# A gap's last product with w_out and the next visit's first product with w_in change places

## The chip, the cores and the metric

The kernel runs on one core of one Trainium2 chip. The metric is the device time of one execution in microseconds. The time before is the median of three runs; the profile is of one execution more.

## The reference

What is computed is an attention with two kinds of masks, followed by two layers of the same form, all in float32. In short:

```python
scores = (q @ k^T) / sqrt(D), masked: 4 heads local (32 keys), 4 heads strided (every 32nd key)
x = softmax(scores) @ v            # 4 x 576 tokens x 512
h = x @ w_in;  x = max(h, 0)**2 @ w_out      # layer 1: 512 -> 2048 -> 512
h = x @ w_in2; x = max(h, 0)**2 @ w_out2     # layer 2, the same shape
```

There are 2304 tokens. The change touches the second layer alone.

## The kernel before

Each float32 operand of a product is split into a high part and a rest, and a product is made as three matmuls: high by high, high by rest, rest by high. The second layer is worked off in blocks of tokens: one of 256 tokens (the narrow block) and then four of 512 (the wide blocks). In the wide blocks a 2 x 2 block product is made with seven products in place of eight, for w_in and for w_out alike.

A wide block runs over eight pairs q of column tiles of w_in (with the rows of w_out that belong to them). `pairs7` (line 1239) lists the 32 pairs (k, q) of the four blocks. `seven` (line 1518) runs over 31 of them and calls `frame` (line 1318) for each: `frame` makes the products with w_in of the pair that comes next (`nxt`) in four *visits*, and between them, in four *gaps*, the products with w_out of the present pair. So TensorE alternates in an order that is written out by hand:

- visit 1: products "11" and "s2" (12 matmuls), then gap 0 (9 matmuls),
- visit 2: product "12" (6 matmuls), then gap 1 (9),
- visit 3: products "s1" and "s3" (12), then gap 2 (15),
- visit 4: products "s4" and "22" (12), then gap 3 (9).

That is 84 matmuls a pair, each 128x128 by 128x256. A visit (`visit`, line 1273; the matmul is line 1279) takes weights as the stationary operand and x (from `xall`) as the moving one, and writes the PSUM tile `ps_m`. There is one such tile for the four visits of a pair, in the pool `ps_h` with one buffer (the third and fourth visit of the first pair of all take another). Its first matmul starts a new sum. After visit 1 ScalarE copies the tile out (line 1359); after visits 2, 3 and 4 VectorE reads it (`add`, lines 1111 and 1112). A gap's product (`n_unit`, line 1290; the matmul is line 1306) takes g, the squared positive part, as stationary operand (`ah`, `al`, `bh`, `bl`) and a unit of w_out from a ring of eight buffers as the moving one, and adds to a PSUM bank `banks[name]`. After the sixth matmul of a unit `ring_load` (line 1250) has SyncE load the ring's buffer with a later unit (line 1253).

The seven units of a pair come in the order of `ORDER` (line 1235): 11, 12, a22t4, s2t2, s1t1, s3t3, s4b22, six matmuls each. `n_unit` returns two closures of three matmuls each, and `seven` cuts the fourteen into the four gaps:

```python
todo = [one for name in ORDER for one in n_unit(k, q, name)]
gaps = todo[:3], todo[3:6], todo[6:11], todo[11:]
```

In the profile `MATMUL` on PE and its `LDWEIGHTS` on PEld are one product; a wait of a product stands at its weight load.

Of the kernel before, what the change touches and what calls it, by code (L numbers as in the profile page):

```python
# [17 lines left out]
P = 128  # L18
# [57 lines left out]
HALF = DM // 2  # L76
# [93 lines left out]
def tile_attention_then_two_mlps(  # L170
# [9 lines left out]
    nc = tc.nc  # L180
# [258 lines left out]
    for i in range(0, half2, 2):  # L439
        n = i + 2 if i + 2 < half2 else None  # L440
# [660 lines left out]
    def high(hi, src):  # L1101
        nc.scalar.activation(out=hi, in_=src, func=AF.Copy)  # L1102
# [95 lines left out]
    def x_op(k, i):  # L1198
        at = (k - NB) % 2 * 10 + 2 * i if i < 5 else 10 + 2 * i
        return [  # L1200
            xall[:, 48 + (at + a) * TB:48 + (at + a + 1) * TB].rearrange("p (c n) -> p c n", c=2)
            for a in range(2)
        ]
# [35 lines left out]
    pairs7 = [(k, q) for k in range(NB + 1, 2 * NB) for q in range(NF // 2)]  # L1239
# [5 lines left out]
    n_use, banks, acc, of = [0], {}, {}, {}  # L1245

    def ring(u):
        return wt["in", 1, 2 * (u % (NF // 2)) + 1][:, 0]
# [18 lines left out]
    def m_weights(q, name):  # L1267
        if name[0] == "s":
            return [t[:, int(name[1]) - 1] for t in s_parts[NF + 2 * q]]
        w = wt["in", 1, 2 * q + int(name[0]) - 1]  # L1270
        return [w[:, int(name[1]) - 1, a] for a in range(2)]

    def visit(k, q, ps, *products):
        for half, (name, i) in enumerate(products):
            w_hi, w_lo = m_weights(q, name)
            x_hi, x_lo = x_op(k, i)
            for j in range(2):
                for m, (w, x) in enumerate(((w_hi, x_hi), (w_lo, x_hi), (w_hi, x_lo))):
                    nc.tensor.matmul(  # L1279
                        ps[:, half * HT:(half + 1) * HT],  # L1280
                        lhsT=w[:, j * P:(j + 1) * P],
                        rhs=x[:, j],
                        start=half == 0 and j == 0 and m == 0,
                        stop=half + 1 == len(products) and j == 1 and m == 2,
                    )
# [4 lines left out]
    def n_unit(k, q, name):  # L1290
        first, end = q == 0, q == NF // 2 - 1
        if k == last7:
            end = q == NF // 2 - 2 and name not in ("12", "s4b22")
        u = n_use[0]
        n_use[0] += 1
        w_hi, w_lo = (ring(u)[:, a] for a in range(2))

        def half(t):
            if first and t == 0:
                tag = BANK.get(name, "a")  # L1300
                pool = ps_a if tag == "a" else ps_y
                banks[name] = pool.tile([P, 512], F32, tag=tag, name="ps_y")
            h, lo = g_op(name)
            rows = slice(t * P, (t + 1) * P)
            for m, (g, w) in enumerate(((h, w_hi), (h, w_lo), (lo, w_hi))):
                nc.tensor.matmul(  # L1306
                    banks[name][:, t * HALF:(t + 1) * HALF],
                    lhsT=g[:, rows],
                    rhs=w,
                    start=first and t == 0 and m == 0,  # L1310
                    stop=end and t == 1 and m == 2,
                )
            if t:
                ring_load(u + NF // 2)

        return [lambda t=t: half(t) for t in range(2)]

    def frame(gaps, nxt, cur, copies=((), (), ()), end=False, x=((), (), ()), late=()):

        k, q = nxt  # L1320
        if not of:
            of["r"] = gpool.tile([P, TB], F32, tag="r", name="r", bufs=1)
            of["c"] = gpool.tile([P, TB], F32, tag="sq", name="c", bufs=1)
            shapes = {"bh": ("qk0", 4), "bl": ("qk1", 4), "ah": ("qk2", 3)}
            for t, (tag, n) in shapes.items():
                of[t] = fpool.tile([P, n * HALF], F32R, tag=tag, name=t, bufs=1).rearrange(
                    "p (i n) -> p i n", i=n)
            for t, n in (("al", 2), ("al2", 1)):
                of[t] = gpool.tile([P, 3 * HALF], F32R, tag="gl", name=t, bufs=2)[
                    :, 48:48 + n * HALF].rearrange("p (i n) -> p i n", i=n)  # L1330
        r, c = (of[t].rearrange("p (h n) -> p h n", h=2) for t in ("r", "c"))
        a11, a22, a21, a12 = r[:, 0], r[:, 1], c[:, 0], c[:, 1]
        ah, al, bh, bl = (of[t] for t in ("ah", "al", "bh", "bl"))
        sums_x, high_x, rest_x = x

        def positive(t, src):
            nc.scalar.activation(out=t, in_=src, func=AF.Relu)
            nc.scalar.activation(out=t, in_=t, func=AF.Square)

        if cur:  # L1340
            s13, s24 = (
                gpool.tile([P, TB + P], F32, tag="gh", name="s", bufs=2)[:, :TB].rearrange(
                    "p (i n) -> p i n", i=2)
                for _ in range(2)
            )
            high(ah[:, 2], a12)
            tt(s13[:, 0], a21, a22, ALU.add)
            tt(s13[:, 1], a11, a21, ALU.subtract)
            rest(ah[:, 2], of["al2"][:, 0], a12)
            tt(s24[:, 0], s13[:, 0], a11, ALU.subtract)  # L1350
            tt(s24[:, 1], a12, s24[:, 0], ALU.subtract)
        each(copies[0])
        ps = ps_h.tile([P, TB], F32, tag="h", name="ps_m")
        visit(k, q, ps, ("11", 0), ("s2", 1))
        m, u = (vpool.tile([P, 512], F32, tag="val", name="u") for _ in range(2))

        c11, u2 = m[:, :HT], m[:, HT:]
        u3 = u[:, HT:]
        nc.scalar.activation(out=m, in_=ps, func=AF.Copy, scale=W_BACK)
        tt(u2, c11, u2, ALU.add)  # L1360
        each(copies[1])
        if cur:
            high(ah[:, 0:2], s13)
            high(bh[:, 2:4], s24)
        each(copies[2])
        each(gaps[0])
        if end:
            first_sum()
            rest(ah[:, 0:2], al, s13)
        visit(k, q, ps, ("12", 2))  # L1370
        add(c11, ps[:, :HT], c11)
        if cur:
            rest(bh[:, 2:4], bl[:, 2:4], s24)
        if cur and not end:
            rest(ah[:, 0:2], al, s13)
        each(sums_x)
        if end:
            each(high_x)
            each(rest_x)
        positive(a11, c11)  # L1380
        high(bh[:, 0], a11)
        if not end:
            each(high_x)
        each(gaps[1])
        if nxt == pairs7[0]:
            ps = ps_a.tile([P, TB], F32, tag="a", name="ps_m")
        visit(k, q, ps, ("s1", 3), ("s3", 4))
        add(
            u.rearrange("p (h n) -> p h n", h=2),
            ps.rearrange("p (h n) -> p h n", h=2),  # L1390
            u2.unsqueeze(1).to_broadcast([P, 2, HT]),
        )
        add(a22, ps[:, :HT], u3)
        positive(a22, a22)
        high(bh[:, 1], a22)
        rest(bh[:, 0], bl[:, 0], a11)
        if not end:
            each(rest_x)
        each(gaps[2])
        each(late)  # L1400
        rest(bh[:, 1], bl[:, 1], a22)
        visit(k, q, ps, ("s4", 5), ("22", 6))
        add(of["c"], ps, u)
        squares(of["c"])
        each(gaps[3])
# [110 lines left out]
            nc.sync.dma_start(out=rows_out(1, 1)[:, a], in_=halves(o)[:, a])  # L1516

    def seven():
        copies, sums = None, []
        for n, (k, q) in enumerate(pairs7[:-1]):  # L1520
            todo = [one for name in ORDER for one in n_unit(k, q, name)]
            gaps = todo[:3], todo[3:6], todo[6:11], todo[11:]
            end = q == NF // 2 - 1 or n + 2 == len(pairs7)
            more = k < last7
            x = [[], [], []]
            if more and q == 0:
                x_work[k + 1] = x_works(k + 1)
            if more and q > 1:
                x = [list(part) for part in x_work[k + 1][q - 2]]
            late = [lambda: sums_late(not more)] if end else []  # L1530
            if sums:
                first, then = sums.pop(0)
                x[0] += first
                late += then
            frame(gaps, pairs7[n + 1], True, copies or ((), (), ()), end, x, late)
            copies = None
            if more and q in (1, 2):
                load_x(k + 1, q - 1)
            if end and more:
                copies, sums = sums_then(k)  # L1540
        finish()
# [8 lines left out]
    with tc.manual_schedule():  # L1550
# [3 lines left out]
        ps = ps_h.tile([P, TB], F32, tag="h", name="ps_w")[:, :P]  # L1554
# [19 lines left out]
        for s in range(len(steps)):  # L1574
            k, f = steps[s]
            layer, j = blocks[k]
# [81 lines left out]
```

## Time and profile before

| | |
|---|---|
| median of 3 runs | 860.36 us (860.15 to 861.51) |
| the profiled execution | 861.31 us, its span 859.5 us |
| PE busy | 847.9 us, 99% of the span |
| PEld busy | 770.0 us, 90% |
| VectorE (DVE) busy | 681.6 us, 79% |
| ScalarE (ACT) busy | 525.8 us, 61% |

The page of the profile has the busy time of each engine, the span in 40 slices with the clock granted to TensorE, and groups of instructions by line. Ends of matmuls are modelled, so a busy PE doesn't say how closely its matmuls follow one another; their starts do. The loop that the change touches runs from about 557 us to 850 us.

### The profile page before, as it was taken

Reading aid. Unit: us, or ns where it says so; the run is one execution under the profiler, and the core shown is the slowest. Engines: PE = TensorE matmul, PEld = TensorE weight load, DVE = VectorE, ACT = ScalarE, POOL = GpSimd, SP = SyncE. Lnnn points to the kernel's source line nnn. Section 1 sums busy time; section 2 is a strip of 40 time slices with the busy share of each in tenths; the row PEclk is TensorE's granted clock in tenths of the full one; section 3 lists DMA queues with packets and bytes.
Section 4 is the critical chain, followed back from the end, with each engine's and each line's share of the span. In section 5 each row is a group of like instructions: output and inputs, shape, how many; then the busy total and the mean of one; then the engine's idle time right before and its main releaser. Section 6 shows DMA issues by size and latency. Waiting matters only on the chain. (4 is left out here: it accounts for less than half of the span.)

```text
span 859.5 us, 16041 instructions
## 1 busy us (share of the span) xinstructions
PE 847.9 (99%) x5719; PEld 770.0 (90%) x5719; DVE 681.6 (79%) x1710; ACT 525.8 (61%) x1216; POOL 17.5 (2%) x15
## 2 busy tenths in 40 slices
PE   8899999999999999999999999999999999999998
PEld 8778888888788888899888899999999999999998
DVE  5899896489775777478889996678888888888877
ACT  6987775467675666376766774455555564556442
POOL 0710000000000000000000000000000000000000
PEclk9999999999999999999999999999999999999999
DMA  8965721222222222268996476476668667766764
GB/s 257 348 216 157 239 64 45 88 78 76 73 78 98 61 71 59 74 245 295 348 364 213 157 265 239 130 225 202 188 202 281 186 194 236 238 187 198 229 188 132
DMA packets 82399, 155.21 MB, mean 181 GB/s; under 512 B 7568, under 2 KB 36368, under 8 KB 80272
## 3 DMA queue, kind: packets, MB, share of 16 engines
q1 hardware_dynamic: 82320, 154.19, 55.1%
q8 instruction: 45, 0.74, 0.3%
q14 instruction: 34, 0.28, 0.1%
HBM read 127.95 MB, written 26.21 MB: 179 GB/s over the span
## 5 line engine op out<-in xcount | busy, mean ns | idle before, releaser
L975 PE MATMUL ps_h<-xall,w 128*128 128x512 f32 (+1 forms) x1153 | 247.3, 358 | 0.0
L975 PEld LDWEIGHTS ps_h<-xall,w 128*128 128x128 f32 x1153 | 185.1, 188 | 26.0
L975 PE MATMUL ps_y<-gh,w 128*128 128x512 f32 (+1 forms) x640 | 155.7, 374 | 0.7 <-ACT gh L1024 0.7
L975 PEld LDWEIGHTS ps_y<-gh,w 128*128 128x128 f32 x640 | 107.9, 188 | 17.6 <-ACT gh L1024 1.1
L1279 PE MATMUL ps_m<-xall,s 128*128 128x256 f32 x768 | 104.5, 279 | 0.3 <-DVE r L1112 0.3
L1018 ACT ACTIVATE r<-ps_h 128x512 f32<-128x512 f32 x80 | 47.7, 597 | 86.9 <-PE ps_h L975 78.1
L1279 PEld LDWEIGHTS ps_m<-xall,s 128*128 128x128 f32 x768 | 95.5, 188 | 0.9 <-DVE r L1112 0.8
L1306 PE MATMUL ps_y<-w,bh 128*128 128x256 f32 x496 | 91.8, 278 | 0.0
L1279 PE MATMUL ps_m<-xall,w 128*128 128x256 f32 x576 | 83.4, 281 | 0.4 <-DVE c L1112 0.4
L975 PE MATMUL ps_y<-gl,w 128*128 128x512 f32 (+1 forms) x324 | 83.8, 370 | 0.0
L1306 PEld LDWEIGHTS ps_y<-w,bh 128*128 128x128 f32 x496 | 75.3, 188 | 0.0
L1279 PEld LDWEIGHTS ps_m<-xall,w 128*128 128x128 f32 x576 | 74.2, 188 | 1.1 <-DVE c L1112 0.6
L1029 DVE TENSOR_TENSOR gl<-sq,gh 128x512 fp32r<-128x512 f32 x80 | 55.3, 691 | 22.2 <-ACT gh L1024 17.5
L1306 PE MATMUL ps_y<-w,ah 128*128 128x256 f32 x372 | 70.0, 278 | 0.0
L1306 PE MATMUL ps_y<-w,bl 128*128 128x256 f32 x248 | 68.8, 277 | 0.0
L1027 DVE TENSOR_TENSOR sq<-r 128x512 f32<-128x512 f32 x38 | 26.3, 692 | 50.6 <-ACT r L1018 50.6
L975 PEld LDWEIGHTS ps_y<-gl,w 128*128 128x128 f32 x324 | 55.7, 188 | 9.6 <-DVE gl L1029 0.4
L1306 PEld LDWEIGHTS ps_y<-w,ah 128*128 128x128 f32 x372 | 56.7, 189 | 0.0
L1112 DVE SCALAR_TENSOR_TENSOR u<-ps_m,u 128x256 f32<-128x256 f32 x64 | 35.7, 557 | 25.5 <-PE ps_m L1279 25.4
L680 ACT ACTIVATE s<-s,m 96x128 f32<-96x128 f32 (+2 forms) x88 | 34.3, 390 | 34.2 <-DVE m L564 33.5
L1102 ACT ACTIVATE ah<-c 128x256 fp32r<-128x256 f32 x33 | 13.7, 418 | 63.4 <-DVE c L1288 63.4
L1306 PE MATMUL ps_y<-w,al 128*128 128x256 f32 x186 | 51.7, 278 | 0.0
(121 smaller groups left out, 1500.8 us busy)
## 6 DMA issues: line engine op xcount, KB each, us to landing
w<-w_mem SPq DMA_DIRECT2D x221, 256.0 KB, 2.8
raw<-moe_w_in_d SPq DMA_DIRECT2D x32, 512.0 KB, 5.7
raw<-moe_w_out_d SPq DMA_DIRECT2D x24, 512.0 KB, 5.2
w_mem<-xall SPq DMA_DIRECT2D x16, 512.0 KB, 3.9
w_mem<-xall SPq DMA_DIRECT2D x8, 1024.0 KB, 5.1
xall<-w_mem SPq DMA_DIRECT2D x8, 1024.0 KB, 5.4
qk<-loc_qk_d SPq DMA_DIRECT2D x12, 416.0 KB, 3.2
out_d<-o SPq DMA_DIRECT2D x17, 256.0 KB, 2.6
```

Source lines behind the costliest of these rows:

```text
L680: nc.scalar.activation(out=blk, in_=blk, func=AF.Exp, scale=-1.0, bias=m[:nq, j:j + 1], accum_out=dens[i][:nq, j:j + 1],)
L975: nc.tensor.matmul(y[:, c:c + w], lhsT=lhsT, rhs=rhs[:, c:c + w], start=start and c == 0, stop=stop and c + w == n,)
L1018: nc.scalar.activation(out=r, in_=ps, func=AF.Relu, scale=W_BACK)
L1027: nc.vector.tensor_tensor(out=sq, in0=r, in1=r, op=ALU.mult)
L1029: nc.vector.tensor_tensor(out=lo, in0=sq, in1=r32(h), op=ALU.subtract)
L1102: nc.scalar.activation(out=hi, in_=src, func=AF.Copy)
L1112: nc.vector.scalar_tensor_tensor(out=dst, in0=src, scalar=sign * W_BACK, in1=to, op0=ALU.mult, op1=ALU.add)
L1279: nc.tensor.matmul(ps[:, half * HT:(half + 1) * HT], lhsT=w[:, j * P:(j + 1) * P], rhs=x[:, j], start=half == 0 and j == 0 and m == 0, sto ...
L1306: nc.tensor.matmul(banks[name][:, t * HALF:(t + 1) * HALF], lhsT=g[:, rows], rhs=w, start=first and t == 0 and m == 0, stop=end and t == 1 ...
```

## The change

`n_unit` returns six closures of one matmul each, in the same order, and `ring_load` stays with the sixth. `seven` cuts the 42 into the same four gaps (9, 9, 15, 9). The last matmul of each gap is taken out of its gap and handed to the next visit as `between`; `visit` issues it after its own first matmul. The last of gap 3 goes to the first visit of the next call. Left as they were: the first visit of the first call (nothing comes from a gap of this loop), the second visit of the first call (`n == 0`), and the last call's gap 3.

```diff
--- before.py
+++ after.py
@@ -1270,12 +1270,14 @@
         w = wt["in", 1, 2 * q + int(name[0]) - 1]
         return [w[:, int(name[1]) - 1, a] for a in range(2)]
 
-    def visit(k, q, ps, *products):
+    def visit(k, q, ps, *products, between=None):
         for half, (name, i) in enumerate(products):
             w_hi, w_lo = m_weights(q, name)
             x_hi, x_lo = x_op(k, i)
             for j in range(2):
                 for m, (w, x) in enumerate(((w_hi, x_hi), (w_lo, x_hi), (w_hi, x_lo))):
+                    if half == 0 and j == 0 and m == 1 and between is not None:
+                        between()
                     nc.tensor.matmul(
                         ps[:, half * HT:(half + 1) * HT],
                         lhsT=w[:, j * P:(j + 1) * P],
@@ -1295,27 +1297,27 @@
         n_use[0] += 1
         w_hi, w_lo = (ring(u)[:, a] for a in range(2))
 
-        def half(t):
-            if first and t == 0:
+        def one(t, m):
+            if first and t == 0 and m == 0:
                 tag = BANK.get(name, "a")
                 pool = ps_a if tag == "a" else ps_y
                 banks[name] = pool.tile([P, 512], F32, tag=tag, name="ps_y")
             h, lo = g_op(name)
-            rows = slice(t * P, (t + 1) * P)
-            for m, (g, w) in enumerate(((h, w_hi), (h, w_lo), (lo, w_hi))):
-                nc.tensor.matmul(
-                    banks[name][:, t * HALF:(t + 1) * HALF],
-                    lhsT=g[:, rows],
-                    rhs=w,
-                    start=first and t == 0 and m == 0,
-                    stop=end and t == 1 and m == 2,
-                )
-            if t:
+            g, w = ((h, w_hi), (h, w_lo), (lo, w_hi))[m]
+            nc.tensor.matmul(
+                banks[name][:, t * HALF:(t + 1) * HALF],
+                lhsT=g[:, t * P:(t + 1) * P],
+                rhs=w,
+                start=first and t == 0 and m == 0,
+                stop=end and t == 1 and m == 2,
+            )
+            if t and m == 2:
                 ring_load(u + NF // 2)
 
-        return [lambda t=t: half(t) for t in range(2)]
-
-    def frame(gaps, nxt, cur, copies=((), (), ()), end=False, x=((), (), ()), late=()):
+        return [lambda t=t, m=m: one(t, m) for t in range(2) for m in range(3)]
+
+    def frame(gaps, nxt, cur, copies=((), (), ()), end=False, x=((), (), ()), late=(),
+              between=(None,) * 4):
 
         k, q = nxt
         if not of:
@@ -1351,7 +1353,7 @@
             tt(s24[:, 1], a12, s24[:, 0], ALU.subtract)
         each(copies[0])
         ps = ps_h.tile([P, TB], F32, tag="h", name="ps_m")
-        visit(k, q, ps, ("11", 0), ("s2", 1))
+        visit(k, q, ps, ("11", 0), ("s2", 1), between=between[0])
         m, u = (vpool.tile([P, 512], F32, tag="val", name="u") for _ in range(2))
 
         c11, u2 = m[:, :HT], m[:, HT:]
@@ -1367,7 +1369,7 @@
         if end:
             first_sum()
             rest(ah[:, 0:2], al, s13)
-        visit(k, q, ps, ("12", 2))
+        visit(k, q, ps, ("12", 2), between=between[1])
         add(c11, ps[:, :HT], c11)
         if cur:
             rest(bh[:, 2:4], bl[:, 2:4], s24)
@@ -1384,7 +1386,7 @@
         each(gaps[1])
         if nxt == pairs7[0]:
             ps = ps_a.tile([P, TB], F32, tag="a", name="ps_m")
-        visit(k, q, ps, ("s1", 3), ("s3", 4))
+        visit(k, q, ps, ("s1", 3), ("s3", 4), between=between[2])
         add(
             u.rearrange("p (h n) -> p h n", h=2),
             ps.rearrange("p (h n) -> p h n", h=2),
@@ -1399,7 +1401,7 @@
         each(gaps[2])
         each(late)
         rest(bh[:, 1], bl[:, 1], a22)
-        visit(k, q, ps, ("s4", 5), ("22", 6))
+        visit(k, q, ps, ("s4", 5), ("22", 6), between=between[3])
         add(of["c"], ps, u)
         squares(of["c"])
         each(gaps[3])
@@ -1516,10 +1518,17 @@
             nc.sync.dma_start(out=rows_out(1, 1)[:, a], in_=halves(o)[:, a])
 
     def seven():
-        copies, sums = None, []
+        copies, sums, kept = None, [], None
         for n, (k, q) in enumerate(pairs7[:-1]):
             todo = [one for name in ORDER for one in n_unit(k, q, name)]
-            gaps = todo[:3], todo[3:6], todo[6:11], todo[11:]
+
+            cuts = 0, 9, 18, 33, 42
+            gaps = [todo[a:b] for a, b in zip(cuts, cuts[1:])]
+            between = [kept] + [gap.pop() for gap in gaps[:3]]
+            if n == 0:
+                gaps[0].append(between[1])
+                between[1] = None
+            kept = gaps[3].pop() if n + 2 < len(pairs7) else None
             end = q == NF // 2 - 1 or n + 2 == len(pairs7)
             more = k < last7
             x = [[], [], []]
@@ -1532,7 +1541,7 @@
                 first, then = sums.pop(0)
                 x[0] += first
                 late += then
-            frame(gaps, pairs7[n + 1], True, copies or ((), (), ()), end, x, late)
+            frame(gaps, pairs7[n + 1], True, copies or ((), (), ()), end, x, late, between)
             copies = None
             if more and q in (1, 2):
                 load_x(k + 1, q - 1)
```

## Rows read from the trace of the kernel before

**Rows 1.** the page: busy us, share and instructions; granted clock in 40 slices

```profile
PE 847.9 (99%) x5719; PEld 770.0 (90%) x5719; DVE 681.6 (79%) x1710; ACT 525.8 (61%) x1216; POOL 17.5 (2%) x15
...
PEclk9999999999999999999999999999999999999999
```

**Rows 2.** the list of waits, 557 to 850 us: who, us in total, times, longest

```profile
PEld ps_m L1279 <- DVE c L1112: 0.6, 1, 0.6
```

**Rows 3.** the timeline of PE, 596 to 606 us: start us, us, line, tiles, count

```profile
596.03 0.85 PE L1279 MATMUL ps_m<-xall,w 128*128 128x256 f32 x6
...
597.41 0.39 PE L1306 MATMUL ps_y<-w,bh 128*128 128x256 f32 x2
...
598.43 0.87 PE L1279 MATMUL ps_m<-xall,w 128*128 128x256 f32 x6
599.14 0.40 PE L1306 MATMUL ps_y<-w,ah 128*128 128x256 f32 x2
...
600.20 1.54 PE L1279 MATMUL ps_m<-xall,s 128*128 128x256 f32 x12
601.57 0.39 PE L1306 MATMUL ps_y<-w,bh 128*128 128x256 f32 x2
...
603.27 0.87 PE L1279 MATMUL ps_m<-xall,s 128*128 128x256 f32 x6
...
604.69 0.40 PE L1306 MATMUL ps_y<-w,ah 128*128 128x256 f32 x2
...
605.75 0.52 PE L1279 MATMUL ps_m<-xall,w 128*128 128x256 f32 x3
```

**Rows 4.** the timeline, two first visits whose weight load waited

```profile
634.10 0.69 DVE L1112 SCALAR_TENSOR_TENSOR c<-ps_m,u 128x512 f32<-128x512 f32 x1
...
634.84 0.77 PEld L1279 LDWEIGHTS ps_m<-xall,w 128*128 128x128 f32 x6
...
732.09 0.68 DVE L1112 SCALAR_TENSOR_TENSOR c<-ps_m,u 128x512 f32<-128x512 f32 x1
...
732.83 0.30 PEld L1279 LDWEIGHTS ps_m<-xall,w 128*128 128x128 f32 x2 [0.64 <-DVE c L1112]
```

**Rows 5.** the timeline, an ordinary first visit: reader of ps_m and weight load

```profile
604.89 0.69 DVE L1112 SCALAR_TENSOR_TENSOR c<-ps_m,u 128x512 f32<-128x512 f32 x1 [0.15 <-PE ps_m L1279]
...
605.64 0.66 PEld L1279 LDWEIGHTS ps_m<-xall,w 128*128 128x128 f32 x5
```

**Rows 6.** the timeline, an ordinary second visit

```profile
597.61 0.60 ACT L1359 ACTIVATE u<-ps_m 128x512 f32<-128x512 f32 x1 [0.57 <-PE ps_m L1279]
...
598.32 0.30 PEld L1279 LDWEIGHTS ps_m<-xall,w 128*128 128x128 f32 x2
```

**Rows 7.** the timeline, an ordinary third and fourth visit

```profile
599.34 0.42 DVE L1112 SCALAR_TENSOR_TENSOR u<-ps_m,u 128x256 f32<-128x256 f32 x1 [0.48 <-PE ps_m L1279]
...
600.09 0.19 PEld L1279 LDWEIGHTS ps_m<-xall,s 128*128 128x128 f32 x1
...
602.50 0.42 DVE L1112 SCALAR_TENSOR_TENSOR r<-ps_m,u 128x256 f32<-128x256 f32 x1
...
603.16 0.30 PEld L1279 LDWEIGHTS ps_m<-xall,s 128*128 128x128 f32 x2
```

**Rows 8.** the timeline, the fourth visit and its gap at a block's end

```profile
632.42 0.65 PEld L1279 LDWEIGHTS ps_m<-xall,s 128*128 128x128 f32 x5
...
633.89 0.39 PE L1306 MATMUL ps_y<-w,ah 128*128 128x256 f32 x2
...
634.92 0.54 PE L1279 MATMUL ps_m<-xall,w 128*128 128x256 f32 x3
```

**Rows 9.** the page's DMA issues: KB each, median us to landing

```profile
w<-w_mem SPq DMA_DIRECT2D x221, 256.0 KB, 2.8
```

**Rows 10.** the timeline of PE, the same gap at another block's end

```profile
711.73 0.40 PE L1306 MATMUL ps_y<-w,ah 128*128 128x256 f32 x2
...
712.79 0.63 PE L1279 MATMUL ps_m<-xall,w 128*128 128x256 f32 x4
```

## The prediction

> **What bounds the kernel now.** I read the busy shares first, then the idle time of the stretch that the change touches, then single starts in it. On the page TensorE (PE) is busy 99% of the span and the clock row shows the full 2.4 GHz level everywhere [rows 1]. So only PE's own spacing, or a hole in its stream, can move the time. The changed loop runs from 557 us to 850 us. There the list of waits has next to nothing for PE: one wait of 0.6 us of a weight load [rows 2]. Every other engine waits for PE, not PE for it.
>
> Single starts show two things that the shares hide. I use starts alone, since ends of matmuls are modelled. A pair of the loop (84 products) runs from the first product of a visit at 596.03 to the same product at 605.75, 9.72 us [rows 3]; this repeats within 0.01 us in most pairs.
>
> First, **PE has two paces.** Differences of starts over counts of products [rows 3]: first visit 1.38 us for 12, its gap 1.02 for 9, second visit 0.71 for 6, its gap 1.06 for 9, third visit 1.37 for 12, its gap 1.70 for 15, fourth visit 1.42 for 12, its gap 1.06 for 9. That is 113 ns a product in a fast stretch and 118 in a slow one, at one granted clock. The pace changes only where a gap ends and a visit begins, there at each of the four visits; from a visit into its gap it stays. So 36 products of 84 run slow (6 + 9 + 12 + 9). At 1.02/9 and 1.06/9 the difference is 4.4 ns, so slow stretches cost 36 x 4.4 = 0.16 us a pair. The rest, 9.72 - 84 x 0.1133 - 0.16 = 0.04 us, lies at the eight borders between visits and gaps, some 5 ns each.
>
> Second, **the first weight load of a visit is hardly early.** A visit's first product overwrites the PSUM tile of the visit before it, so its weight load waits until VectorE or ScalarE has read that tile. How long after the reader's end the load can start is seen where it had to wait: reader 634.10 + 0.69 = 634.79, load 634.84; and 732.09 + 0.68 = 732.77, load 732.83 [rows 4]. I take 0.05 us. In the ordinary pair, first visit: reader 604.89 + 0.69 = 605.58, load 605.64: 0.06 us, so no slack that I can read [rows 5]. Second visit: ScalarE 597.61 + 0.60 = 598.21, load 598.32: slack 0.11 - 0.05 = 0.06 [rows 6]. Third: 599.34 + 0.42 = 599.76, load 600.09: slack 0.28. Fourth: 602.50 + 0.42 = 602.92, load 603.16: slack 0.19 [rows 7].
>
> **The change part by part.** No product, load, DMA or byte is added or removed; the products of a gap are cut one by one instead of by threes, which changes no instruction. In a pair with all swaps the order at four places goes from "gap's last, visit's first, visit's second" to "visit's first, gap's last, visit's second". Swapped are the third and fourth visit of 31 pairs and the first and second of 30 (the first pair has no gap of the loop ahead of it and its second visit is left alone; the last pair's closing gap feeds no visit): 122 places.
>
> *What the swap does to the wait.* The last product of a visit keeps its place, so the tile's reader starts and ends as before. The load of the next visit's first product moves up by one product, and everything behind it on PE's queue (the gap's product and the visit's rest) stands behind its wait.
> - First visit: its load moves up by one slow product, 0.12 us, from 605.64 to 605.52 [rows 5]; it can go at 605.58 + 0.05 = 605.63. Wait 0.11 us x 30 = 3.3 us. In the blocks' first pairs a wait is there already (634.84 above); there the same 0.11 is added, so the count stands.
> - Second visit: it moves up by one fast product, 0.11, from 598.32 to 598.21, and can go at 598.21 + 0.05 = 598.26 [rows 6]: 0.05 us x 30 = 1.5 us. If its gap ran slow, the gap would be 0.04 longer, and 0.01 would be left.
> - Third and fourth: slack 0.28 and 0.19 against 0.11, so nothing [rows 7]. At the end of a block the fourth already waits: its twelve products take from about 632.43 (load 632.42) to 633.89, 1.46 us, some 0.1 more than the 1.37 of a fast twelve [rows 3, 8]. Three such places, 0.11 each: 0.3 us.
> Sum of waits: 5.1 us. What hides an earlier product elsewhere is only this slack; there is no other work for PE behind a waiting load.
>
> *What else moves.* The gap's product that is passed ends up to 0.11 us later, plus the wait. Two of the four (ahead of visits three and one) carry the issue of the weight ring's next DMA on SyncE; the ring holds eight units and a pair uses seven, so the unit loaded is used more than a pair later, over 9.7 us, and a load lands in 2.8 us [rows 9], so nothing waits. The passed product's g operand has 0.11 us more time. VectorE and ScalarE follow PE, and shift with it.
>
> *What it does to the paces.* No row of before shows a single visit product between two gap products, so I bound it. At best all products run at the fast pace: minus 0.16 us a pair and minus the slips at the changes. At worst all run slow: 48 x 4.4 ns = plus 0.21 us. In between lies "as many slow as now": 0. What rows say of the middle: a fourth visit that began after a wait was followed by a fast gap once (633.89 to 634.92, 1.03 for 9) and at the next block's end by a slow one (711.73 to 712.79, 1.06 for 9) [rows 8, 10]. So a wait doesn't settle the pace. I take 0, the middle, since the swap makes two borders of the flipping kind out of one, and rows speak neither for a lasting fast pace nor for a lasting slow one. Borders: 122 places each get two more; at 5 ns a border [rows 3] that is 1.2 us; bounds 0 (the borders inside a wait are hidden) and 2.4 us (twice that for a visit of one product).
>
> By the Trainium skill ("TensorE: Matmul & The Clock Gate", section "Back-to-back issue gap") a warm product of 256 columns follows the last after 256/2.4 + 2.5 = 109 ns. The trace's two paces, 113 and 118, both lie above it, and by that rule there would be one pace only, nothing to win or lose in it: the sum would be the waits alone, plus 5.1 us.
>
> **Sum.** 5.1 (waits) + 0 (paces) + 1.2 (borders) = 6.3 us on top of the profiled execution's 861.31 us (span 859.5 and 1.8 around it). The three runs have the median 860.36 with 861.51 as the highest, so the profiled one was among the slower; I add the 6.3 to the median: 866.7.
>
> **The rivals.**
> *All fast with the waits.* If the swap, or the waits themselves, keep PE at the fast pace, a pair loses 0.16 and some 0.02 of slips. But a faster gap brings the load of the first visit earlier still: in the fast gap at 633.89 the load waited 0.04 without any swap [rows 4, 8], so the waits are 0.15 and 0.05. Then 9.72 - 0.18 + 0.20 + 0.04 (borders) = 9.78: plus 0.06 x 30 + 0.3 = 2.1 us, 862.5; without cost for borders 861.3. For it: after the wait at 632.42 the pace stayed fast through a border at which it flips elsewhere [rows 8, 10]. Against: at every border from gap to visit without a wait in the pair the pace flips [rows 3].
> *All slow.* If each passing pair of flips ends on the slow side: 0.21 on the pair, waits 0.11 and 0.01, borders 0.04: 0.37 x 30 + 0.3 = 11.4 us, 871.8. The flip at each such border, twice now at each swap, would hold whatever pace the unswapped visit leaves, and that one goes from fast to slow, as at 598.43 [rows 3].
> *Faster.* One mechanism: the steady fast pace wins more than the waits cost. Place: the third and fourth visits and their gaps, where no wait arises (48 products, 21 of them slow now) and the other slow stretches. Price: 0.18 us a pair against the waits. It decides at waits of less than 0.14 in all, for a gain of 0.2%: if the first visit's wait is 0.11 and the second's hidden, with borders free, 0.07 x 30 = 2.1 us faster, 858.3. Against it: the first visit's reader is on a chain that starts with the visit's last product and is as long as before, and in a fast gap its wait is 0.15.
> *It does nothing*: the waits are as said but half of them are paid back by the pace; within 1.7 us of 860.4. It shares its range with the first rival.
>
> **How the numbers follow.** A measurement here can tell about 0.2%, 1.7 us, from no change. Chances: forecast (waits, paces mixed) 0.52, between 863.5 and 869; all fast with waits 0.2, half of it within 1.7 us; all slow 0.15; nothing 0.06; faster 0.07. So faster 0.07, same 0.16, slower 0.77. The range leaves out the faster case and the last of the slow one: 861.0 to 871.5.
>
> **What would show it.** Right: in the loop the weight load of the first visit's first product starts 0.05 us after VectorE's last read of the visit tile in every pair, with some 0.1 us in which PE runs nothing; that of the second visit the same after ScalarE's read, some 0.05; third and fourth don't wait. The pair is 9.85 to 10.0 us long instead of 9.72, and stretches of both paces are still there. Wrong: a pair of 9.72 or less; first-visit loads that don't wait; or one pace throughout, which decides between 862 and 872.

## The result and the profile after

The changed kernel takes 866.89 us (866.43 to 866.95, four runs) against 860.78 us (860.15 to 861.51) for the kernel before in the same measurement: the ratio is 1.007, 95% interval 1.0052 to 1.0087. That is 6.1 us more; 6.3 us were predicted. Its profiled execution took 866.43 us, its span is 864.6 us. The span grew by 5.1 us only. The one long wait of [rows 2] (the load at 732.83 in [rows 4], 0.7 us late by exact starts) is in the profile of before and not in that of after; the other 0.3 us are less than the runs of one kernel differ by.

In the changed file the visit's matmul is line 1281 (1279 before), the gap's matmul 1307 (1306), the copy by ScalarE 1361 (1359). The page, with total busy time, granted clock and the groups of the visit's products (busy us, mean ns of one, idle time before them):

```profile
PE 854.2 (99%) x5719; PEld 774.5 (90%) x5719; DVE 682.7 (79%) x1710; ACT 525.3 (61%) x1216; POOL 17.6 (2%) x15
...
PEclk9999999999999999999999999999999999999999
...
L1281 PE MATMUL ps_m<-xall,w 128*128 128x256 f32 x576 | 94.1, 287 | 0.0
...
L1281 PEld LDWEIGHTS ps_m<-xall,w 128*128 128x128 f32 x576 | 78.1, 188 | 2.6 <-ACT u L1361 0.4
```

The same number of products stands at the same clock as in [rows 1], and PE is still "99% busy". The list of waits of the loop has no entry for a weight load or a product now, where before it had that of one product [rows 2]. So the views that add up idle time hide the 6 us: a weight load of 188 ns reaches past a short wait, and the modelled end of a matmul (0.39 us here) does too. The time is counted as busy (854.2 us against 847.9), and only starts tell where it lies. The timeline of PE over the pair that answers to [rows 3]:

```profile
596.44 0.39 PE L1281 MATMUL ps_m<-xall,w 128*128 128x256 f32 x1
...
598.04 0.39 PE L1307 MATMUL ps_y<-w,bh 128*128 128x256 f32 x2
...
598.95 0.33 PE L1281 MATMUL ps_m<-xall,w 128*128 128x256 f32 x1
...
599.82 0.39 PE L1307 MATMUL ps_y<-w,ah 128*128 128x256 f32 x2
...
600.72 0.28 PE L1281 MATMUL ps_m<-xall,s 128*128 128x256 f32 x1
...
602.25 0.40 PE L1307 MATMUL ps_y<-w,bh 128*128 128x256 f32 x2
...
603.91 0.28 PE L1281 MATMUL ps_m<-xall,s 128*128 128x256 f32 x1
...
605.41 0.39 PE L1307 MATMUL ps_y<-w,ah 128*128 128x256 f32 x2
...
606.36 0.39 PE L1281 MATMUL ps_m<-xall,w 128*128 128x256 f32 x1
```

The pair is 9.92 us long instead of 9.72 (26 of the 30 that lie between two gaps of the loop are within 0.01 us of that). An exchanged visit carries the passed product in its stretch, so a visit and its gap are best taken together (us, from exact starts, which the timeline rounds):

| stretch (products) | before | after | |
|---|---|---|---|
| first visit and gap 0 (21) | 2.39 | 2.51 | +0.12 |
| second visit and gap 1 (15) | 1.77 | 1.77 | 0.00 |
| third visit and gap 2 (27) | 3.07 | 3.18 | +0.11 |
| fourth visit and gap 3 (21) | 2.48 | 2.45 | -0.03 |

Some of the loss stands where no load waits: the third visit and gap 2 went over to the slow pace (602.25 to 603.91 is 118.6 ns a product for 14), while gaps 1 and 3 became fast (599.82 to 600.72 is 112.5 ns for 8). Now the waits, in the timeline: the reader of `ps_m` and the load behind it, at the first visit,

```profile
605.61 0.69 DVE L1112 SCALAR_TENSOR_TENSOR c<-ps_m,u 128x512 f32<-128x512 f32 x1 [0.20 <-PE ps_m L1281]
...
606.09 0.39 PE L1307 MATMUL ps_y<-w,bh 128*128 128x256 f32 x2
...
606.36 0.19 PEld L1281 LDWEIGHTS ps_m<-xall,w 128*128 128x128 f32 x1
...
606.58 0.28 PE L1307 MATMUL ps_y<-w,bl 128*128 128x256 f32 x1
```

at the second,

```profile
598.24 0.60 ACT L1361 ACTIVATE u<-ps_m 128x512 f32<-128x512 f32 x1 [0.68 <-PE ps_m L1281]
...
598.72 0.39 PE L1307 MATMUL ps_y<-w,ah 128*128 128x256 f32 x2
...
598.89 0.19 PEld L1281 LDWEIGHTS ps_m<-xall,w 128*128 128x128 f32 x1
```

and at the third and fourth:

```profile
600.02 0.42 DVE L1112 SCALAR_TENSOR_TENSOR u<-ps_m,u 128x256 f32<-128x256 f32 x1 [0.65 <-PE ps_m L1281]
...
600.61 0.19 PEld L1281 LDWEIGHTS ps_m<-xall,s 128*128 128x128 f32 x1
...
603.18 0.42 DVE L1112 SCALAR_TENSOR_TENSOR r<-ps_m,u 128x256 f32<-128x256 f32 x1
...
603.79 0.19 PEld L1281 LDWEIGHTS ps_m<-xall,s 128*128 128x128 f32 x1
```

An unhindered load starts with the product before it. At the first visit that product (the second of the two at 606.09) starts at 606.20; the reader ends at 606.30 and the load comes at 606.36: 0.15 us late by the exact starts, in nearly every pair. From 606.20 the passed product at 606.58 is 0.38 us away, where two fast products take 0.23. At the second visit the reader ends at 598.84, the load comes at 598.89 instead of 598.83: 0.055 late. At the third and fourth the load comes 0.17 and 0.19 after the reader's end, just with the product before it: no wait.

### The profile page after: what moved, and what is told of

Its sections match the earlier page's. It is cut to its first block, busy times and chain, and to the rows that moved or that the text cites. A ratio compares the mean times of both kernels' runs of the same rounds, so it can differ in the third digit from the quotient of the medians.

```text
span 864.6 us, 16043 instructions
## 1 busy us (share of the span) xinstructions
PE 854.2 (99%) x5719; PEld 774.5 (90%) x5719; DVE 682.7 (79%) x1710; ACT 525.3 (61%) x1216; POOL 17.6 (2%) x15
## 5 line engine op out<-in xcount | busy, mean ns | idle before, releaser
L1281 PE MATMUL ps_m<-xall,s 128*128 128x256 f32 x768 | 112.9, 280 | 0.3 <-DVE r L1112 0.3
L1281 PEld LDWEIGHTS ps_m<-xall,s 128*128 128x128 f32 x768 | 101.0, 188 | 0.9 <-DVE r L1112 0.8
L1281 PE MATMUL ps_m<-xall,w 128*128 128x256 f32 x576 | 94.1, 287 | 0.0
L1281 PEld LDWEIGHTS ps_m<-xall,w 128*128 128x128 f32 x576 | 78.1, 188 | 2.6 <-ACT u L1361 0.4
```

The source lines that it names most:

```text
L1281: nc.tensor.matmul(ps[:, half * HT:(half + 1) * HT], lhsT=w[:, j * P:(j + 1) * P], rhs=x[:, j], start=half == 0 and j == 0 and m == 0, sto ...
```

## The experiments

Two questions: is it the waits that cost, and what do the paces do? Three theories stood in the expectations. **Waits**: each exchange costs as much as its first load comes late. **Border**: the pace flips where a gap ends and a visit begins, whatever lies in between. **Count**: the flip hangs on how many products (odd or even) lie between. Medians of the kernel before were 860.71 us beside `swap_first`, `swap_third`, `swap_fourth` and `even_cuts`, 860.81 beside `short_reader`, `first_by_two`, `swap_even` and `upper_first`, and 860.68 beside `swap_second`, `short_waits` and `all_swapped`. An interval is of the ratio to it.

**One exchange at a time.** `between` is built so that one visit alone takes a product of its gap:

```diff
-            between = [kept] + [gap.pop() for gap in gaps[:3]]
+            between = [kept, None, None, None]
```

(That is `swap_first`; `swap_second`, `swap_third` and `swap_fourth` fill the one other place and set `kept = None`.)

> Of the exchange only the one at the first visit is left; visits two, three and four are as before. Theory of the waits: the first visit's load waits 0.11 us in each of 30 pairs, PE runs nothing in that time, all else as before: 9.82 us a pair, about 863.9 us. Rival, that the exchange costs by its borders and the pace and the wait is hidden: two more borders, 0.01 us a pair, 9.73 and 861.2 us.

Measured: 864.54 us, ratio 1.0042 (1.0027 to 1.0057), pair 9.83 to 9.85 us. Timeline of its first visit:

```profile
605.38 0.69 DVE L1112 SCALAR_TENSOR_TENSOR c<-ps_m,u 128x512 f32<-128x512 f32 x1 [0.15 <-PE ps_m L1281]
...
605.89 0.40 PE L1307 MATMUL ps_y<-w,bh 128*128 128x256 f32 x2
606.12 0.19 PEld L1281 LDWEIGHTS ps_m<-xall,w 128*128 128x128 f32 x1
```

The reader ends at 606.07, the load comes at 606.12, 0.117 late: gap 3 is still slow here, and the wait is the slow product that was passed. All the paces are those of before. Here the loss, 0.11 to 0.13 us a pair, is the wait and nothing else.

> The exchange at the second visit alone, from the second pair on. Theory of the waits: its load waits 0.05 us in each pair, and a visit that begins after a wait stays fast; the third visit then turns slow and the fourth fast, so the gap ahead of the first visit is fast and its load waits 0.04 there. 27 slow products in place of 36: 9.72 - 0.04 - 0.01 + 0.09 + 0.01 = 9.77 us a pair, 862.3 us. Rival, that a wait does nothing to the pace: the second visit slow as before, 9.79 us and 862.8 us; the paces of the stretches tell the two apart, the time hardly.

Measured: 863.21 us, 1.003 (1.0018 to 1.0042), pair 9.78 to 9.80 us.

```profile
597.68 0.60 ACT L1361 ACTIVATE u<-ps_m 128x512 f32<-128x512 f32 x1 [0.56 <-PE ps_m L1281]
...
598.33 0.19 PEld L1281 LDWEIGHTS ps_m<-xall,w 128*128 128x128 f32 x1
```

The load comes 0.05 after ScalarE's read, 0.056 late. After that wait gap 1 is fast, the third visit and gap 2 are slow, the fourth visit and gap 3 fast: the order of the changed kernel. And since gap 3 is fast, the first visit's load, which nobody moved, is 0.038 late. So the shift of the paces comes with the second visit's wait, and a fast gap 3 alone costs a first visit 0.04.

> Of the exchange only the one at the third visit is left, where no load has to wait. Theory of the count: the border that counts is the last one, ahead of the visit's second product; it lies 16 products after the second visit's first, an even number, so the third visit, its gap, and (26 later) the fourth visit stay slow: 63 slow products of 84, 9.84 us a pair, about 864.4 us. Theory of the border, one flip a visit however it begins: paces as before, 9.73 us a pair and 861.2 us. No wait by either.

> Of the exchange only the one at the fourth visit is left. Theory of the count: its last border lies 28 products after the third visit's first, so the fourth visit and its gap stay fast; a fast gap brings the first visit's load 0.04 us too early, a wait as in the first pairs of the blocks before; the first visit stays fast, the second is slow as before: 15 slow products of 84, 9.66 us a pair, about 859.0 us, faster than both kernels. Theory of the border, one flip a visit: paces as before, no wait, 9.73 us a pair and 861.2 us.

Measured: 860.99 us (1.0003, 0.9994 to 1.0013) and 861.17 us (1.0005, 0.9995 to 1.0014), pairs 9.73 and 9.72 us. Timeline of PE in the first of them:

```profile
600.48 0.40 PE L1307 MATMUL ps_y<-w,ah 128*128 128x256 f32 x2
...
601.42 0.28 PE L1281 MATMUL ps_m<-xall,s 128*128 128x256 f32 x1
...
601.66 1.43 PE L1281 MATMUL ps_m<-xall,s 128*128 128x256 f32 x11
602.92 0.39 PE L1307 MATMUL ps_y<-w,bh 128*128 128x256 f32 x2
```

The gap runs at 117.5 ns a product (0.94 for 8), the visit's eleven at 114.5 (1.26 for 11): slow turns into fast as it did at this visit before. An exchange whose load doesn't wait is free, and it flips the pace once, as an unexchanged border does. The count theory expected 864.4 and 859.0 here, and both fall.

**Other cuts, no exchange** (gaps of 10, 8, 14 and 10 products):

```diff
-            cuts = 0, 9, 18, 33, 42
+            cuts = 0, 10, 18, 32, 42
```

> No product is exchanged with a visit; only the cuts between the gaps are moved, from 9, 9, 15 and 9 products to 10, 8, 14 and 10. So from the first product of one visit to the first of the next there are 22, 14, 26 and 22 products, all even, where before they were 21, 15, 27 and 21. Theory of the count: the pace changes at a border from gap to visit when an odd number of products lies between two such borders and stays when it is even. Then the pace no longer changes in a pair; fast throughout gives 84 x 0.1133 plus some 0.02 for borders, 9.54 us a pair instead of 9.72, and about 855.3 us; slow throughout would give 9.9 and about 866. Theory of the border: each such border flips the pace, whatever the count. Then two visits of four are slow as before, 9.72 us a pair and 860.8 us. By both no visit waits except in a block's first pair: the load of the first visit has one product more of the gap ahead of it.

Measured: 863.13 us, 1.0029 (1.0016 to 1.0042), pair 9.81 us: neither number. Timeline of PE:

```profile
597.58 0.40 PE L1307 MATMUL ps_y<-w,bh 128*128 128x256 f32 x2
...
598.76 0.87 PE L1281 MATMUL ps_m<-xall,w 128*128 128x256 f32 x6
599.47 0.28 PE L1307 MATMUL ps_y<-w,ah 128*128 128x256 f32 x1
...
600.41 1.54 PE L1281 MATMUL ps_m<-xall,s 128*128 128x256 f32 x12
601.79 0.39 PE L1307 MATMUL ps_y<-w,bh 128*128 128x256 f32 x2
```

The gap of 10 from 597.58 is slow (1.18 us), and the visit after it stays slow (0.71 for 6); after the gap of 8 the visit is fast (1.38 for 12). The pace stayed slow at 55 of 58 borders behind a slow gap of 10, so the border theory holds for fast to slow, not always for slow to fast. No load waits in these stretches, yet the kernel is 2.4 us slower: the paces alone (22 more slow products a pair) are worth this much.

**The same products, upper half first.** The visit takes `for j in (1, 0)`, so the first load of a visit reads the other half.

> No exchange; a visit's product takes the upper half of its contraction first, then the lower. The first weight load of a visit then reads 512 bytes further on in its tile. If the flip of the pace where a gap ends and a visit begins hangs on where the first load reads against the matmul that runs beside it, it goes or comes elsewhere: fast throughout would be 9.58 us a pair with a wait of 0.04 at the first visit, about 856.5 us; slow throughout 9.9, 866 us. If it hangs on the border as such: paces as before, 9.72 us a pair and 860.8 us.

Measured: 860.73 us, 1.0001 (0.9991 to 1.001), pair 9.72, the paces as before. Which half of the contraction the visit's first load reads doesn't matter.

**The changed kernel with a shorter reader.** VectorE's read after the fourth visit takes half of `ps_m` only; the fourth visit's second product is left out of the result.

```diff
-        add(of["c"], ps, u)
+        add(of["c"][:, :HT], ps[:, :HT], u[:, :HT])
+        tt(of["c"][:, HT:], u[:, HT:], u[:, :HT], ALU.add)
```

> The changed kernel, but VectorE's add after the fourth visit reads only the first 256 of the 512 columns of the visit's tile (the other half is made from SBUF; the fourth visit's second product is left out of the result). The tile is free some 0.27 us sooner, so the first visit's load has nothing to wait for; order and count of the products are those of the changed kernel. Theory of the waits: the 0.15 us a pair at the first visit go; what remains is 0.05 at the second visit and the flips of the pace: 9.72 to 9.82 us a pair, 861 to 864 us. Rival, that the exchanged products themselves cost: 9.92 us a pair, 866.9 us.

Measured: 863.38 us, 1.0032 (1.0021 to 1.0044), pair 9.80 us.

```profile
605.76 0.42 DVE L1112 SCALAR_TENSOR_TENSOR c<-ps_m,u 128x256 f32<-128x256 f32 x1 [0.20 <-PE ps_m L1281]
...
606.24 0.39 PE L1307 MATMUL ps_y<-w,bh 128*128 128x256 f32 x2
606.36 0.19 PEld L1281 LDWEIGHTS ps_m<-xall,w 128*128 128x128 f32 x1
606.47 0.28 PE L1281 MATMUL ps_m<-xall,w 128*128 128x256 f32 x1
```

The reader ends at 606.18 and the load stands at 606.36 with the product before it: no wait, 0.15 us less. But without the wait the first visit and gap 0 turn slow, at some 118 ns a product (21 products, 4.4 ns each: 0.09 us back), which in turn makes the second visit's load only 0.02 late. Net 0.12 of the 0.20 us a pair goes. This is the same exchange with the reader out of the way, so the reader's end is what the exchange runs into.

**Two products passed at the first visit alone.**

```diff
+            two = [gaps[3].pop() for _ in range(2)][::-1] if n + 2 < len(pairs7) else None
+            kept = (lambda two=two: each(two)) if two else None
```

> The exchange at the first visit alone, but its first product goes ahead of the last two products of the gap. Theory of the waits: one product more of wait, 0.113 us a pair on top of the exchange with one product (9.84 us a pair, 864.5 us): 9.95 us a pair, 867.9 us. Rival, that the cost is that of the borders: no difference to the exchange with one, 864.5 us.

Measured: 869.79 us, 1.0106 (1.0091 to 1.0121), pair 9.99 to 10.03 us.

```profile
607.13 0.69 DVE L1112 SCALAR_TENSOR_TENSOR c<-ps_m,u 128x512 f32<-128x512 f32 x1 [0.16 <-PE ps_m L1281]
...
607.88 0.19 PEld L1281 LDWEIGHTS ps_m<-xall,w 128*128 128x128 f32 x1 [0.17 <-DVE c L1112]
```

The load again comes 0.06 after the reader's end and is now 0.236 late behind a slow gap, 0.263 behind a fast one: one product more than in `swap_first`, as expected. The wait is long enough that the trace names it. The 1.9 us beyond the expected 867.9 lie in the paces: behind this longer wait the first visit and gap 0 run slow in 25 of 30 pairs, where in `swap_first` they are fast in all 30. Such a pair, from first visit to first visit, is 10.02 to 10.05 us long; where they stay fast it is 9.96 (10.01 at a change of block), close to the expected 9.95. So a wait doesn't always leave a fast pace behind it.

**All exchanges with the even cuts.** The changed kernel with gaps of 10, 8, 14 and 10.

> The changed kernel with the exchange at all four visits of every pair but the first visit of the first, and with the cuts 10, 8, 14 and 10 in place of 9, 9, 15 and 9, so that the loads of the first and the second visit stand behind nine products of their gap, as in the kernel before. Theory of the waits: no wait at the second visit, at the first none after a slow gap and 0.04 us after a fast one; third and fourth keep some slack. 9.72 to 9.80 us a pair, 861 to 863.5 us. Rival, the exchange itself costs: 9.9 us a pair and 866 to 867 us.

Measured: 861.78 us, 1.0013 (1.0004 to 1.0023), pair 9.71 to 9.77, up to 10.0 around the changes of block.

```profile
604.64 0.69 DVE L1112 SCALAR_TENSOR_TENSOR c<-ps_m,u 128x512 f32<-128x512 f32 x1
...
605.24 0.39 PE L1307 MATMUL ps_y<-w,bh 128*128 128x256 f32 x2
605.39 0.19 PEld L1281 LDWEIGHTS ps_m<-xall,w 128*128 128x128 f32 x1
```

With one product more in gaps 0 and 3 the first load is 0.04 late and the second not at all. The exchanges are as many as in the changed kernel, and 5 of its 6 us are gone. The waits alone don't account for this. What is saved at the first and second visit is 0.165 us a pair, 5.0 us in all. Gap 2 has one product less here, and the fourth visit's load is now 0.04 us late, which takes 1.3 us back. In most pairs only 14 products run slow, against 27 in the changed kernel; over the loop that gives some 1 us by my estimate.

**Short waits on purpose.** The kernel before, without exchange, with gaps of 9, 11, 13 and 9, so that the first and fourth visit wait a little and keep the fast pace.

> No exchange; the cuts are 9, 11, 13 and 9, so the fourth visit's load comes two products earlier than before and waits some 0.04 us. Theory that a border from gap to visit turns a fast pace slow unless the load waits there: the fourth visit and its gap stay fast, the first visit's load waits 0.04 and stays fast too; only the second visit and its gap are slow, 17 products: 9.72 - 0.08 - 0.02 + 0.08 = 9.70 us a pair, 860 us, no difference that the times can show, but three of four visits fast. Rival, a short wait does not keep the pace: 36 slow products or more, 9.76 us or more a pair, 862 us.

Measured: 862.6 us, 1.0025 (1.0014 to 1.0035), pairs 9.73 to 9.74 us, up to 10.0 around the changes of block. Timeline of PE:

```profile
604.33 0.90 PE L1281 MATMUL ps_m<-xall,s 128*128 128x256 f32 x6
605.07 0.84 PE L1281 MATMUL ps_m<-xall,w 128*128 128x256 f32 x6
605.75 0.39 PE L1307 MATMUL ps_y<-w,ah 128*128 128x256 f32 x2
```

The gaps behind the waits were fast, but the first six products behind a wait took 0.74 us (123 ns each with the wait in them), which eats the gain in an ordinary pair. Most of the 1.9 us lost lies in eleven pairs around the changes of block, 9.79 to 10.01 us long. No version that I tried beats the kernel before.

**The exception taken out**: the second visit of the first pair is exchanged too.

> The changed kernel without its exception: the second visit of the first pair is exchanged too. There the load waits some 0.09 us already, so it waits 0.2 us: 0.1 us more, once; all later pairs as in the changed kernel, 9.92 us, and the time 867.0 us. If the exception sets the pace for the pairs that follow, they would differ by up to 0.2 us each.

Measured: 866.75 us (one run), mean pair 9.930 us against 9.931 of the changed kernel. The exception touches the first pair alone and makes no difference to the mean of the later ones. The wait of 0.2 us that was expected there didn't come: that load is 0.03 us late.

## Why the prediction was right, and where its steps were off

**The total was right, and its main mechanism is shown**: first and second visit wait for the reader of `ps_m`, third and fourth don't, both paces are still there, and a pair takes 9.92 us, within the 9.85 to 10.0 named. Singly, the exchanges cost 0.11 to 0.13, 0.06 to 0.08, about 0.01 and 0.00 us a pair; the sum of 0.18 to 0.22 holds the 0.20 measured together. Thirty pairs at 0.20 are 6.0 us.

**The terms, a pair.**

| | predicted | measured |
|---|---|---|
| first visit's wait | 0.11 | 0.15 |
| second visit's wait | 0.05 | 0.055 |
| paces | 0 | -0.04 |
| borders | 0.04 | 0.035 (what is left of 0.20) |

*First visit: mis-sized.* I priced it from [rows 5], where gap 3 is slow. After the change gap 3 is fast and brings the load 0.038 earlier still; I had that number, 0.15, only in the rival "all fast". `swap_first`, with a slow gap 3, shows the predicted 0.117. The step should have said: the price hangs on the pace of gap 3.

*Paces: right for a wrong reason.* I wrote that an exchange "makes two borders of the flipping kind out of one". It doesn't: `swap_third` and `swap_fourth` flip once at their exchanged visit. What happens is that the wait at the second visit keeps the fast pace across one border, and all later flips come out the other way round. Slow before were the second and fourth visit and gaps 1 and 3 (36 products); slow after are the third visit and gap 2 (27). Nine products at 4.4 ns are the 0.04 us given back. It offsets the larger first wait to the hundredth, by chance: a total that fits didn't prove its terms.

*The blocks' first pairs: over-sized, and named wrongly.* I added 0.3 us for three places "at the end of a block". In the timeline of PE of before, the loop starts at

```profile
547.25 0.87 PE L1279 MATMUL ps_m<-xall,w 128*128 128x256 f32 x6
```

and not at 557, so 632.43 [rows 8] is in the ninth pair, the first of a block. There the fourth load was 0.1 us late before and is 0.10 to 0.11 late after: gap 2 runs slow now and pays for most of the exchange. These three pairs grew from 9.75, 9.81 and 9.78 to 10.01 us, on average 0.03 more than the others: 0.1 us in all.

*The look of a wait.* I expected some 0.1 us in which PE runs nothing. No view shows that; what shows it is the load's start beside its reader's end (0.05 to 0.06 us behind it, as taken from [rows 4]) and the distance between starts.

**The rivals.** *All slow* falls: 27 products of 84 are slow. *All fast* had the right first wait and the wrong paces. *Faster* needed waits below 0.14 us in all; they are 0.205. *Does nothing* supposed that the paces pay back half of the waits; they pay back a fifth. The Trainium skill ("TensorE: Matmul & The Clock Gate", section "Back-to-back issue gap") has one spacing of warm products by its formula, 109 ns for 256 columns, and gives the formula for an isolated product; for a stream of weight loads and products it has figures at 128 and 512 columns alone. The trace doesn't agree with one spacing: the stream here has two paces, 113 and 118 ns. With one pace the sum would have been the predicted waits alone, 5.1 us.

**Open**: why the pace flips. Odd or even counts (`swap_third`, `swap_fourth`) and the half that is read first (`upper_first`) are out as causes, and the clock is granted in full all along. Why a slow gap of 10 isn't followed by a fast visit where one of 8 or 9 mostly is (in `first_by_two` 7 of 25 second visits behind a slow gap of 9 stayed slow too), and why a wait keeps the fast pace in one place and not in another, no run settles.

## What to carry to other kernels

A product that overwrites a tile can be moved up only by the time between the end of the tile's last reader and its load, less the 0.05 us that a load came behind its reader here; read both from starts, under the pace that the stretch will have after the change, since the lists of idle time show nothing of the waits of 0.055 and 0.15 us here. A load that waits holds everything behind it on the engine, so in a stream at 99% each such wait is paid as often as the loop runs, less or more what the paces behind it change. Try the places of a change one by one: two of these four were free and two cost everything.

## What the runs showed of the hardware that I had not expected

At one granted clock TensorE's products of 256 columns, each with its own weight load, follow each other at 113.3 or at some 118 ns, and hold a pace for whole stretches. Where a gap gave over to a visit without a wait, a fast pace turned slow at nearly every border: 58 of 58 before, 31 of 31 after. A slow one turned fast at 57 of 57 before, but at 3 of 58 behind gaps of 10 (`even_cuts`). A wait of 0.055 or 0.15 us at the border kept the fast pace in 59 of 59 cases after. Other waits didn't always: fast turned slow in 15 of 20 cases behind 0.26 us (`first_by_two`), in 3 of 3 behind 0.17 us (`even_cuts`), and in one of three behind 0.1 us in before [rows 10]. Where the second visit's wait of 0.055 us was the one new thing at a border (`swap_second`), the paces of some 60 products behind it came out the other way round.
